# Half of the first MLP product by seven half-size products instead of eight, in blocks 1 to 8

## The chip, the cores and the metric

The kernel runs on one core of one Trainium2 chip. The metric is the device time of one execution in microseconds (us). Three runs before the change took 303.65, 304.41 and 304.56 us, with the median at 304.41 us. The core's engines are named as the profile names them: PE is the matrix engine (TensorE; PEld is its loading of weights), DVE is VectorE, ACT is ScalarE, POOL is GpSimd, and SP issues transfers. SBUF is the on-chip memory. PSUM is the memory into which PE writes its products; the kernel divides it into banks of 512 float32 values in each of 128 partitions.

## What is computed

Sparse attention over 8 batches, 8 heads, 576 positions and head size 64 (four heads with a local window, four with a strided pattern) gives `attn_out`. After it stands an MLP over 4608 tokens, with `d_model` 512 and `d_ff` 2048:

```python
x = attn_out.transpose(0, 2, 1, 3).reshape(B * S, H * D)   # 4608 x 512
h = x @ w_in                                               # MLP1, 512 -> 2048
sp = np.where(h > 20.0, h, np.log1p(np.exp(np.minimum(h, 20.0))))
g = h * np.tanh(sp)                                        # Mish
return (g @ w_out).astype(np.float32)                      # MLP2, 2048 -> 512
```

## The kernel before

Tokens are worked in nine blocks of 512 (`t` = 0 to 8, loop at L758). A block has two stages on PE. In **MLP1** (`mlp1`, L453) a group `g` makes two chunks of 128 rows of `h` transposed: 4 matmuls of 128x512 for each chunk, so 8 for a group, 64 for a block (L473). Mish follows on ACT straight from PSUM into `gT` (L483 for a pair of chunks, L479 for one chunk). In block 4 the 512 tokens wrap around the ring buffer `xT`, so its matmuls are twice as many and half as wide. In **MLP2** of blocks 1 to 8 (`mlp2_seven`, L519, and `mlp2_last`, L588) the product is already made by the Strassen-Winograd scheme: the matrices are cut in quarters, and seven products of quarters with sums of quarters replace eight. Its sums of `g` (`sums_g`, L499, four DVE instructions for a range of chunks, into `Sg`) are made as chunks of `gT` appear, and its sums of `w_out` (`sums_w`, L509, four instructions, into `Tw`) once, in block 1, right after the first piece of MLP1 (L787). Block 0 uses plain products in both stages.

The attention of batch `t + 1` is cut into steps and laid out by hand between the steps of MLP2 of block `t` (`attn_steps`, L391; the list `at` is run at L803). From batch 4 on a few of its last steps go into MLP1 of the next block (`late`, L440). The attention output reaches `xT` by PE transposes and an ACT copy (`xt`, L364): cc 2 and 3 of `xT` hold the strided heads (`X("s", ...)`), cc 0 and 1 the local ones (`X("l", ...)`), which come last.

Everything stands under one manual schedule: each engine takes its instructions in the order in which the program emits them, and an instruction waits until the data and buffers it needs are free. PSUM is divided for blocks 1 to 8 into `acc0` and `acc1` of two banks each, `bank0` and `bank1` of one bank each, and two banks for transposes and small products. MLP1 goes around acc0, acc1 and the bank pair (L460 to L467), so a buffer comes back after two other groups. Of the steps of block 0, the last (`at[15]`, L764) puts on DVE's queue the spreading of V (`spread_v_str`) behind the last attention work, and on POOL's queue the casts of V.

## Time and profile before

| what | before |
|---|---|
| median of 3 runs | 304.41 us |
| the profiled execution, its own time | 303.47 us |
| its span in the profile | 301.7 us |
| MLP1 of block 1, 2, 4, 5, 8, first matmul to the first of MLP2 | 13.94, 13.82, 14.48, 14.11, 13.81 us |
| MLP2 of block 1, 2 (with attention of the next batch) | 17.32, 17.45 us |
| in MLP1 of block 1: DVE, ACT, POOL busy | 11.37, 10.15, 5.61 us |
| in MLP1 of block 2: DVE, ACT, POOL busy | 4.72, 8.26, 2.67 us |

The profile is of one execution, with times from the start of its span. In a row of the timeline stand start, duration, engine, line, operation, what is written and read, the shape, and how many instructions are merged. In a group's row the two numbers behind the bar are busy time in us and the mean of one instruction in ns; behind the next bar stands the idle time of the engine before these instructions and what ended it. Records of matmuls overlap: one of 128x512 shows 379 ns, but the next one starts 216 ns later. What a matmul costs is read from starts.

### The profile page before, as it was taken

The page shows a single profiled execution, that of the slowest core. Times are in us where ns is not written, and L with a number is a line of the kernel's source. Part 1 is how long each engine was busy: PE and PEld are TensorE (multiplying, and loading weights), DVE is VectorE, ACT ScalarE, POOL GpSimd, SP SyncE. Part 2 cuts the span into 40 slices and gives each one's busy share as a digit, 9 for nine tenths or more (in the row PEclk, how much of TensorE's full clock was granted, in tenths as well). Part 3 has the DMA queues.
Part 4 walks back from the last instruction along what each step waited for, and adds up shares of the span by engine and source line. Part 5 has one row for each costly group of instructions (what it writes and reads, how often), then busy time and mean ns, then how long its engine had stood idle before and what let it go on. Part 6 is the DMA issues. An engine that isn't in the chain of part 4 may idle for free.

```text
span 301.7 us, 6848 instructions
## 1 busy us (share of the span) xinstructions
PE 293.5 (97%) x2900; PEld 198.4 (66%) x2921; DVE 156.4 (52%) x356; ACT 171.8 (57%) x220; POOL 108.1 (36%) x116
## 2 busy tenths in 40 slices
PE   8999999999999999999999999999999999999995
PEld 3654555546874688458899885478646864684484
DVE  2360266978561766095617662676348544620732
ACT  1677634587646765567556855675467636404620
POOL 8285302535581239141934085206620510000000
PEclk9999999999999999999999999999999999999999
DMA  8999999969999999999779976994590030003003
GB/s 157 187 202 200 194 197 195 180 132 200 253 156 177 286 175 137 122 272 171 110 133 277 165 94 107 280 146 77 80 243 0 3 141 0 2 0 141 0 0 141
DMA packets 103738, 43.25 MB, mean 143 GB/s; under 512 B 86172, under 2 KB 99212, under 8 KB 103708
## 3 DMA queue, kind: packets, MB, share of 16 engines
q1 hardware_dynamic: 86620, 30.05, 55.9%
q0 software_dynamic: 16800, 12.51, 27.7%
q8 instruction: 23, 0.38, 0.5%
q10 hardware_dynamic: 288, 0.25, 0.3%
q14 instruction: 7, 0.06, 0.1%
HBM read 38.38 MB, written 9.44 MB: 159 GB/s over the span
## 4 chain that ended last, share of the span: by engine, by line
PE 92%; DVE 4%; ACT 2%; issue 1%; ACTq 0%
PE psh L473 32%; PE pso L545 27%; PE psb L473 9%; PE po L333 4%; PE pso L573 4%; PE pso L600 4%; PE ps L303 4%; PE un L257 3%; PE trx L372 2%; PE trx L382 1%; DVE x_l L359 1%; DVE osb L524 1%; PE tr L229 1%; ACT Pl L311 1%; PE tr L243 1%
## 5 line engine op out<-in xcount | busy, mean ns | idle before, releaser
L473 PE MATMUL psh<-xT,w_in 128*128 128x512 bf16 (+1 forms) x484 | 100.7, 358 | 0.8
L473 PEld LDWEIGHTS <-w_in 128*128 128x128 bf16 x640 | 61.5, 98 | 58.3 <-issue 0.8
L483 ACT ACTIVATE gT<-psh 128x1024 bf16<-128x1024 f32 x56 | 56.3, 1023 | 45.4 <-PE psh L473 43.0
L497 DVE TENSOR_TENSOR Sg<-gT 128x256 bf16<-128x256 bf16 (+2 forms) x64 | 29.8, 471 | 50.9 <-ACT gT L483 48.7
L545 PEld LDWEIGHTS <-Sg 128*128 128x128 bf16 x448 | 41.9, 98 | 6.3
L317 POOL TENSOR_TENSOR Pl<-Pl,consts_sb 128x960 bf16<-128x960 bf16 (+1 forms) x18 | 29.2, 1633 | 46.1 <-ACT Pl L311 46.1
L545 PE MATMUL pso<-Tw,Sg 128*128 128x256 bf16 x336 | 40.1, 273 | 0.0
L182 POOL CAST vl<-vl 128x768 bf16<-128x768 f32 x15 | 13.7, 939 | 59.0 <-DMA vl<-in_v_dram 50.5
L545 PEld LDWEIGHTS <-gT 128*128 128x128 bf16 x336 | 31.4, 98 | 4.6
L180 ACT COPY xT<-trx 128x576 bf16<-128x576 bf16 x32 | 20.2, 641 | 19.5 <-PE trx L382 13.6
L473 PE MATMUL psb<-xT,w_in 128*128 128x512 bf16 (+1 forms) x141 | 30.1, 355 | 0.2
L180 ACT COPY osb<-pso 128x512 f32<-128x512 f32 (+1 forms) x26 | 14.2, 545 | 26.4 <-PE pso L545 16.1
L545 PE MATMUL pso<-w_out,gT 128*128 128x256 bf16 x224 | 27.8, 273 | 0.0
L524 DVE TENSOR_TENSOR osb<-pso,osb 128x512 f32<-128x512 f32 x21 | 14.5, 692 | 21.4 <-PE pso L545 21.4
L311 ACT ACTIVATE Pl<-ps 128x960 bf16<-128x960 f32 (+1 forms) x24 | 19.3, 808 | 11.0 <-PE ps L303 10.8
L311 ACT ACTIVATE Ps<-ps 72x864 bf16<-72x864 f32 (+1 forms) x24 | 18.6, 804 | 5.3 <-PE ps L303 5.1
L479 ACT ACTIVATE gT<-psb 128x512 bf16<-128x512 f32 x32 | 19.0, 597 | 2.9 <-PE psb L473 2.5
L359 DVE TENSOR_TENSOR x_s<-po,rden 72x512 bf16<-72x512 f32 x28 | 19.2, 687 | 1.0
L573 PE MATMUL pso<-w_out,gT 128*128 128x512 bf16 x59 | 15.8, 380 | 0.5 <-issue 0.3
L497 DVE TENSOR_TENSOR Sg<-Sg,gT 128x256 bf16<-128x256 bf16 (+2 forms) x32 | 15.6, 488 | 1.1
L344 DVE RECIPROCAL rden<-po 96x4 f32<-96x4 f32 (+1 forms) x22 | 3.9, 178 | 22.1 <-PE po L333 22.0
L333 PEld LDWEIGHTS <-Ps 72*128 72x128 bf16 x256 | 12.1, 97 | 5.0 <-DVE Ps L317 1.9
(89 smaller groups left out, 347.0 us busy)
## 6 DMA issues: line engine op xcount, KB each, us to landing
out_dram<-osb SPq DMA_DIRECT2D x16, 512.0 KB, 6.1
vl<-in_v_dram SPq DMA_DIRECT2D x7, 768.0 KB, 7.4
kl<-in_k_dram SPq DMA_DIRECT2D x6, 576.0 KB, 9.3
ql<-in_q_dram SPq DMA_DIRECT2D x6, 576.0 KB, 13.7
qs<-in_q_dram POOLq DMA_DIRECT2D x8, 288.0 KB, 11.3
vsr<-in_v_dram POOLq DMA_DIRECT2D x8, 288.0 KB, 7.3
w_in<-in_moe_w_in_dram POOLq DMA_DIRECT2D x4, 512.0 KB, 9.7
w_out<-in_moe_w_out_dram POOLq DMA_DIRECT2D x4, 512.0 KB, 17.1
```

The lines of the kernel that those rows point to most:

```text
L180: nc.scalar.copy(out_, in_)
L311: nc.scalar.activation(pt[0:n, :, 0:nw], ps[0:n, :, o0:o0 + nw], AF.Exp, scale=scale)
L317: meng.tensor_tensor(out=pm, in0=pm, in1=mk[0:n, :].unsqueeze(1).unsqueeze(1).to_broadcast([n, 2, nu, w]), op=ALU.mult,)
L333: nc.tensor.matmul(po[:, h, :], lhsT=pt[0:n, c0:c0 + 128], rhs=rhs, start=True, stop=True,)
L359: nc.vector.tensor_tensor(out=dst.rearrange("p e (h d) -> p e h d", h=4), in0=po[0:m, :, :, 0:D], in1=rden[0:m].unsqueeze(3).to_broadcast( ...
L473: nc.tensor.matmul(ps_u[:, o:o + n], lhsT=w_in[:, cc, fc * 128:(fc + 1) * 128], rhs=xT[:, cc, a:a + n], start=(cc == 2 and (o == 0 or len( ...
L479: nc.scalar.activation(gT[:, g + 8 * u, :], ps_u[:], AF.Mish)
L483: nc.scalar.activation(to, tiles[g][:], AF.Mish)
L497: nc.vector.tensor_tensor(out=out_, in0=in0, in1=in1, op=op)
L524: add = lambda o, p: nc.vector.tensor_tensor(out=o, in0=p, in1=o, op=ALU.add)
L545: nc.tensor.matmul(ps[:, pair, :], lhsT=lhs(c, 128 * pair), rhs=rhs(c), start=(first and pair == 0 and c == 0), stop=(last and c == 7), sk ...
L573: nc.tensor.matmul(p[:, ot % 2, :], lhsT=gT[:, fc, 128 * ot:128 * ot + 128], rhs=w_out[:, fc, :], start=(fc == 0), stop=(fc == 15),)
```

## The change

The eight chunks 2 to 5 and 10 to 13 of each block's MLP1 are made by the seven-product scheme, and the other eight by plain groups 0, 1, 6 and 7 as before. The four-chunk *units* are two (n = 0 and 1: chunks 2, 3, 10, 11 and 4, 5, 12, 13). A unit's product is 4 matmuls of 128x256. The two units advance side by side through five stages: `one`, `five`, `two`, `three`, `four`; stage two has two products and stage three has two. Their partial results stay in PSUM: z1 in acc0, z3 in acc1, z2 in the bank pair, and p5 in SBUF. ACT copies z1 to z2 within PSUM, DVE copies z3 to p5 and adds z2 and p5 twice for each unit. The plain group 0 runs between stages two and three. The weights' sums (`sums_w_in`) are made once, at the end of block 0's steps, and three of the four sums of `w_out` are moved to the same place, both ahead of the first of the sums of x for block 1; the fourth sum of `w_out` goes to the last group of block 1. The sums of x (`sums_x`, four DVE instructions of 128x512 for each block) are split: the first in the MLP2 before, the others in MLP1. The sums of `g` are put in another order, and some of them are moved behind the first products of MLP2. To make room, the second buffers of `ql` and `kl` share the memory of `Sw`, later casts and transposes use the first buffer alone, and `Tw` loses a quarter.

```diff
-    ql = [const.tile([128, CL, 4, D], BF16, name=f"ql{i}") for i in range(2)]
-    kl = [const.tile([128, CL, 4, D], BF16, name=f"kl{i}") for i in range(2)]
+    Sw = const.tile([128, 3, 2, 512], BF16, name="Sw")
+    Sx = const.tile([128, 4, 2, 256], BF16, name="Sx")
+    halves = Sw[:].rearrange("p a b c -> p (a b c)").rearrange(
+        "p (z j h d) -> p z j h d", z=2, j=CL, h=4
+    )
+    ql = [const.tile([128, CL, 4, D], BF16, name="ql0"), halves[:, 0]]
+    kl = [const.tile([128, CL, 4, D], BF16, name="kl0"), halves[:, 1]]
...
-    Tw = const.tile([128, 4, 8, 256], BF16, name="Tw")
+    Tw = const.tile([128, 3, 8, 256], BF16, name="Tw")
...
-            to = by_tile(dst[b % 2])
+            to = by_tile(dst[0])
...
-            late = {0: [V("l", 4)], 1: [V("l", 5)], 5: [X("l", 1)]}
+            late = {4: [V("l", 4), V("l", 5)], 6: [X("l", 1)]}
...
-    SUMS_AT = {3: (0, 4), 5: (4, 6), 6: (6, 7), 7: (7, 8)}
-                if t > 0 and g in SUMS_AT:
-                    sums_g(gT, Sg, *SUMS_AT[g])
...
+        z = {}
+
+        def banks():
+            z2 = [bank(u, "psb") for u in range(2)]
+            z1, z3 = [acc(accs[u], "psu") for u in range(2)]
+            p5 = o_pool.tile([128, 2, DM], F32, tag="osb", name="p5")
+            for n in range(2):
+                z[n] = z1[:, n, :], z2[n][:], z3[:, n, :], p5[:, n, :]
+
+        def unit(n):
+
+            f0 = 256 * n
...
+            a11, a12, s3, a22 = [w_quarter(i, j) for i in range(2) for j in range(2)]
+            s1, s2, s4 = [Sw[:, i] for i in range(3)]
+            b11, _, b21, b22 = [x_quarter(t, i, j) for i in range(2) for j in range(2)]
+            t1, t2, t3, t4 = [Sx[:, i] for i in range(4)]
+
+            def product(ps, lhs, rhs, first=False, last=False):
+                for j in range(2):
+                    for cc in range(2):
+                        nc.tensor.matmul(
+                            ps[:, 256 * j:256 * j + 256], lhsT=lhs[:, cc, f0 + 128 * j:f0 + 128 * j + 128],
+                            rhs=rhs[:, cc], start=(first and j == 0 and cc == 0),
+                            stop=(last and cc == 1), skip_group_check=True,
+                        )
+
+            def mish(src, half_f, half_t):
+                c = 8 * half_f + (U0 + f0) // 128
+                nc.scalar.activation(
+                    gT[:, c:c + 2, 256 * half_t:256 * half_t + 256],
+                    src.rearrange("p (j n) -> p j n", j=2), AF.Mish,
+                )
+
+            def one():
+                z1, z2, z3, p5 = z[n]
+                product(z1, a11, b11, first=True)
+                nc.scalar.copy(z2, z1)
+
+            def five():
+                z1, z2, z3, p5 = z[n]
+                product(z3, s1, t1, first=True)
+                nc.vector.tensor_copy(p5, z3)
+
+            def two():
+                z1, z2, z3, p5 = z[n]
+                product(z1, a12, b21, last=True)
+                mish(z1, 0, 0)
+                product(z2, s2, t2)
+                sums(z3, z2, p5, ALU.add)
+
+            def three():
+                z1, z2, z3, p5 = z[n]
+                product(z2, s3, t3)
+                product(z3, s4, b22, last=True)
+                sums(p5, z2, p5, ALU.add)
+                mish(z3, 0, 1)
+                mish(p5, 1, 1)
+
+            def four():
+                z2 = z[n][1]
+                product(z2, a22, t4, last=True)
+                mish(z2, 1, 0)
+
+            return one, five, two, three, four
+
+        one, five, two, three, four = zip(unit(0), unit(1))
+
+        def begin():
+            banks()
+            for f in one:
+                f()
+            sums_x(t, "2")
+            for f in five:
+                f()
+
+        def second():
+            for f in two:
+                f()
+            sums_x(t, "3")
+            sums_x(t, "4")
+
+        def third():
+            for f in three:
+                f()
+
+        def fourth():
+            for f in four:
+                f()
+
+        def plain(g):
+            group(g)
+            if g == 1:
+                sums_g(gT, Sg, 2, 6)
+            if g == 6:
+                sums_g(gT, Sg, 0, 2)
+                sums_g(gT, Sg, 6, 7, "1")
+            if g == 7:
+                if t < B - 1:
+                    nc.scalar.preload_act_table(AF.Exp)
+                if t == 1:
+                    sums_w_last()
+                sums_g(gT, Sg, 7, 8, "1")
+
+        return gT, Sg, [begin, second, lambda: plain(0), third, fourth] + [
+            lambda g=g: plain(g) for g in (1, 6, 7)
+        ]
...
-    def sums_g(gT, Sg, c0, c1):
...
+    def tw_of(i):
+
+        return Tw[:, (0, 1, None, 2)[i]] if i != 2 else w_out[:, 0:8, 256:512]
 
+        sums(tw_of(0), b12, b11, ALU.subtract)
+        sums(tw_of(1), b22, tw_of(0), ALU.subtract)
+        sums(tw_of(3), b21, tw_of(1), ALU.subtract)
+
+    def sums_w_last():
+
+        sums(tw_of(2), w_out[:, 8:16, 256:512], w_out[:, 0:8, 256:512], ALU.subtract)
+
+    U0, U1 = 256, 768
+    GROUP_ACC = {0: 0, 1: 0, 6: 1, 7: 0}
+
+    def w_quarter(i, j):
+
+        return w_in[:, 2 - 2 * j:4 - 2 * j, U0 + 1024 * i:U1 + 1024 * i]
+
+    def sums_w_in():
+
+        a11, a12, a21, a22 = [w_quarter(i, j) for i in range(2) for j in range(2)]
+        s1, s2, s4 = [Sw[:, i] for i in range(3)]
+        sums(s1, a21, a22, ALU.add)
+        sums(s2, s1, a11, ALU.subtract)
+        sums(s4, a12, s2, ALU.subtract)
+        sums(a21, a11, a21, ALU.subtract)
+
+    def x_quarter(t, i, j):
+
+        a = (512 * t + 256 * j) % RT
+        return xT[:, 2 - 2 * i:4 - 2 * i, a:a + 256]
+
+    def sums_x(t, which):
+
+        b11, b12, b21, b22 = [x_quarter(t, i, j) for i in range(2) for j in range(2)]
+        t1, t2, t3, t4 = [Sx[:, i] for i in range(4)]
+        if "1" in which:
+            sums(t1, b12, b11, ALU.subtract)
+        if "2" in which:
+            sums(t2, b22, t1, ALU.subtract)
+        if "3" in which:
+            sums(t3, b22, b12, ALU.subtract)
+        if "4" in which:
+            sums(t4, b21, t2, ALU.subtract)
...
+        steps += product(
+            za, g(0, 0), w(0, 0), True, False,
+            lambda: (cast(nc.vector, c11, za), rest("2")()), late=True,
+        )
+        steps += product(zc, sg(0), tw(0), True, False, lambda: (cast(nc.scalar, c22, zc), rest("4")()))
+        steps += product(za, sg(1), tw(1), False, False, lambda: (cast(nc.scalar, c12, za), rest("3")()))
...
         product(0, g(0, 0), w(0, 0), True, False, lambda n, p: cast(nc.vector, c(0, 0, n), p), late=True)
+        sums_g(gT, Sg, 6, 8, "234")
         product(1, sg(0), tw(0), True, False, lambda n, p: cast(nc.scalar, c(1, 1, n), p))
...
                 at[12].append(load_rest2)
                 at[15] += [
                     lambda: spread_v_str(2, Dv), lambda: cast_v_loc(2, Po),
-                    lambda: load_qk_str(3), lambda: load_early_v_str(3),
+                    lambda: load_qk_str(3), lambda: load_early_v_str(3), sums_w_in, sums_w, lambda: sums_x(1, "1"),
                 ]
...
+                if t + 1 < B:
+                    at[12].append(lambda: sums_x(t + 1, "1"))
...
-                if t == 1 and i == 0:
-                    sums_w()
...
+                if t + 1 == B:
+                    steps[12] = lambda f=steps[12]: (sums_x(t + 1, "1"), f())
```

More of the change, by code (lines that the diff above doesn't have):

```diff
@@ L207, in transpose_by_dma @@
                     dst.rearrange("c (i n) -> c i n", i=NW),
-                    by_tile(src[b % 2])[:, hp].rearrange("p i e d -> p (i e d)"),
+                    by_tile(src[0])[:, hp].rearrange("p i e d -> p (i e d)"),
                 )
@@ L457, in mlp1, with group @@
         held, tiles = {}, {}
-        def group(g, ccs=(2, 3, 0, 1)):
-            single = t > 0 and g % 3 == 2
+        def group(g, ccs=(2, 3, 0, 1), ps=None):
             if g not in held:
-                if single:
-                    held[g] = [bank(u, "psb") for u in range(2)]
-                else:
-                    ps = acc(accs[g % 3], "psh")
-                    held[g] = [ps[:, u, :] for u in range(2)]
-                    tiles[g] = ps
+                if ps is None:
+                    tiles[g] = acc(accs[g % 3 if t == 0 else GROUP_ACC[g]], "psh")
+                    ps = [tiles[g][:, u, :] for u in range(2)]
+                held[g] = ps
             for u in range(2):
@@ L477, in group @@
                         )
-                if ccs[-1] == 1 and single:
-                    nc.scalar.activation(gT[:, g + 8 * u, :], ps_u[:], AF.Mish)
-            if ccs[-1] == 1:
-                if not single:
-                    to = gT[:, g::8, :] if t > 0 else gT[:, 2 * g:2 * g + 2, :]
-                    nc.scalar.activation(to, tiles[g][:], AF.Mish)
-                if t < B - 1 and g == 7:
+                if ccs[-1] == 1 and g not in tiles:
+                    nc.scalar.activation(gT[:, g + 8 * u, :], ps_u, AF.Mish)
@@ L485, in group, with first_group @@
+            if ccs[-1] == 1 and g in tiles:
+                to = gT[:, g::8, :] if t > 0 else gT[:, 2 * g:2 * g + 2, :]
+                nc.scalar.activation(to, tiles[g][:], AF.Mish)
+        if t == 0:
+            def first_group(g):
+                group(g)
+                if g == 7:
                     nc.scalar.preload_act_table(AF.Exp)
-                if t > 0 and g in SUMS_AT:
-                    sums_g(gT, Sg, *SUMS_AT[g])
-        if t == 0:
             halves = [[lambda g=g, c=c: group(g, c) for g in range(3)] for c in ((2, 3), (0, 1))]
-            return gT, halves[0], halves[1] + [lambda g=g: group(g) for g in range(3, 8)]
@@ L491, in mlp1 @@
-        first = [lambda: [group(*x) for x in ((0, (2, 3)), (1, (2, 3)), (0, (0, 1)))], lambda: group(1, (0, 1))]
-        return gT, Sg, first + [lambda g=g: group(g) for g in range(2, 8)]
-    SUMS_AT = {3: (0, 4), 5: (4, 6), 6: (6, 7), 7: (7, 8)}
+            return gT, halves[0], halves[1] + [lambda g=g: first_group(g) for g in range(3, 8)]
+        z = {}
[5 more added lines that the diff above has]
+                z[n] = z1[:, n, :], z2[n][:], z3[:, n, :], p5[:, n, :]
@@ new lines, in plain @@
+        def plain(g):
+            group(g)
+            if g == 1:
[3 more added lines that the diff above has]
+                sums_g(gT, Sg, 6, 7, "1")
+            if g == 7:
+                if t < B - 1:
[6 more added lines that the diff above has]
+        ]
@@ L496, in sums, with sums_g @@
     def sums(out_, in0, in1, op):
         nc.vector.tensor_tensor(out=out_, in0=in0, in1=in1, op=op)
-    def sums_g(gT, Sg, c0, c1):
+    def sums_g(gT, Sg, c0, c1, which="1234"):
         lo1, lo2 = gT[:, c0:c1, 0:256], gT[:, c0:c1, 256:512]
@@ L503, in sums_g @@
         s1, s2, s3, s4 = [Sg[:, i, c0:c1, :] for i in range(4)]
-        sums(s1, lo2, hi2, ALU.add)
-        sums(s2, s1, lo1, ALU.subtract)
-        sums(s4, hi1, s2, ALU.subtract)
-        sums(s3, lo1, lo2, ALU.subtract)
+        if "1" in which:
+            sums(s1, lo2, hi2, ALU.add)
+        if "2" in which:
+            sums(s2, s1, lo1, ALU.subtract)
+        if "3" in which:
+            sums(s3, lo1, lo2, ALU.subtract)
+        if "4" in which:
+            sums(s4, hi1, s2, ALU.subtract)
+    def tw_of(i):
+        return Tw[:, (0, 1, None, 2)[i]] if i != 2 else w_out[:, 0:8, 256:512]
     def sums_w():
@@ L512, in sums_w @@
         b21, b22 = w_out[:, 8:16, 0:256], w_out[:, 8:16, 256:512]
-        t1, t2, t3, t4 = [Tw[:, i] for i in range(4)]
-        sums(t1, b12, b11, ALU.subtract)
-        sums(t2, b22, t1, ALU.subtract)
-        sums(t3, b22, b12, ALU.subtract)
-        sums(t4, b21, t2, ALU.subtract)
+        sums(tw_of(0), b12, b11, ALU.subtract)
[20 more added lines that the diff above has]
+        t1, t2, t3, t4 = [Sx[:, i] for i in range(4)]
+        if "1" in which:
+            sums(t1, b12, b11, ALU.subtract)
+        if "2" in which:
+            sums(t2, b22, t1, ALU.subtract)
+        if "3" in which:
+            sums(t3, b22, b12, ALU.subtract)
+        if "4" in which:
+            sums(t4, b21, t2, ALU.subtract)
     def mlp2_seven(t, gT, Sg, za, zc):
@@ L535, in tw @@
         def tw(i):
-            return lambda c: Tw[:, i, c, :]
+            return lambda c: tw_of(i)[:, c, :]
         def store(h):
@@ L554, in mlp2_seven @@
         cp = lambda eng, o, p: (lambda: cast(eng, o, p))
+        rest = lambda which: (lambda: sums_g(gT, Sg, 6, 8, which))
         steps = []
-        steps += product(za, g(0, 0), w(0, 0), True, False, cp(nc.vector, c11, za), late=True)
-        steps += product(zc, sg(0), tw(0), True, False, cp(nc.scalar, c22, zc))
-        steps += product(za, sg(1), tw(1), False, False, cp(nc.scalar, c12, za))
+        steps += product(
[4 more added lines that the diff above has]
+        steps += product(za, sg(1), tw(1), False, False, lambda: (cast(nc.scalar, c12, za), rest("3")()))
         steps += product(zc, sg(3), w(1, 1), False, True, lambda: add(c12, zc))
@@ L622, in tw @@
         def tw(i):
-            return lambda c: Tw[:, i, c, :]
+            return lambda c: tw_of(i)[:, c, :]
         def done(n, p):
```

## The prediction

> **What bounds the kernel now.** First the page, engines and the chain that ended last:

> ```profile
> PE 293.5 (97%) x2900; PEld 198.4 (66%) x2921; DVE 156.4 (52%) x356; ACT 171.8 (57%) x220; POOL 108.1 (36%) x116
> ...
> PE 92%; DVE 4%; ACT 2%; issue 1%; ACTq 0%
> ```

> PE is the bound nearly everywhere: what shortens its stream shortens the kernel, and what makes it wait lengthens it. The other engines have room on average, so the question is where PE waits. Next the groups of instructions, forms apart (the number before the second bar is the mean in ns):

> ```profile
> L483 ACT ACTIVATE gT<-psh 128x1024 bf16<-128x1024 f32 x56 | 56.3, 1023 | 45.4 <-PE psh L473 43.0 <-PE po L333 2.3
> L479 ACT ACTIVATE gT<-psb 128x512 bf16<-128x512 f32 x32 | 19.0, 597 | 2.9 <-PE psb L473 2.5
> L524 DVE TENSOR_TENSOR osb<-pso,osb 128x512 f32<-128x512 f32 x21 | 14.5, 692 | 21.4 <-PE pso L545 21.4
> L180 ACT COPY osb<-pso 128x512 f32<-128x512 f32 x21 | 12.3, 586 | 16.7 <-PE pso L545 16.1
> ```

> These price the new work: a 128x512 Mish 0.60 us, an addition from PSUM 0.69, a copy 0.59. The timeline of PE in the last block gives the matmul of 128x256:

> ```profile
> 285.90 1.91 PE L600 MATMUL pso<-w_out,gT 128*128 128x256 bf16 x16
> 287.65 3.66 PE L600 MATMUL pso<-Tw,Sg 128*128 128x256 bf16 x32
> 291.14 1.91 PE L600 MATMUL pso<-w_out,Sg 128*128 128x256 bf16 x16
> ```

> From 287.65 to 291.14 are 32 matmuls: 0.109 us each. MLP1 of block 2, 64 of 128x512 in 13.82 us, gives 0.216 each. Last, the passage from block 0 to block 1, first DVE, then PE, then ACT:

> ```profile
> 56.54 0.42 DVE L345 TENSOR_TENSOR x_l<-po,rden 96x256 bf16<-96x256 f32 x1
> 56.88 0.80 DVE L182 COPY vs<-vsr 72x2048 bf16<-72x2048 bf16 x1
> 57.60 1.21 DVE L497 TENSOR_TENSOR Tw<-w_out 128x2048 bf16<-128x2048 bf16 x1
> 58.84 1.73 DVE L497 TENSOR_TENSOR Tw<-w_out,Tw 128x2048 bf16<-128x2048 bf16 x1
> 60.49 1.84 DVE L497 TENSOR_TENSOR Tw<-w_out 128x2048 bf16<-128x2048 bf16 x1
> 62.25 1.84 DVE L497 TENSOR_TENSOR Tw<-w_out,Tw 128x2048 bf16<-128x2048 bf16 x1
> 65.70 0.69 DVE L497 TENSOR_TENSOR Sg<-gT 128x1024 bf16<-128x1024 bf16 x1 [1.61 <-ACT gT L483]
> ```

> ```profile
> 57.41 3.72 PE L473 MATMUL psh<-xT,w_in 128*128 128x512 bf16 x16
> ```

> ```profile
> 60.35 1.28 ACT L483 ACT_TABLE_LOAD   x1 [1.16 <-PE psh L473]
> ```

> DVE goes from attention work straight into the sums of w_out and is busy to 64.1, yet PE starts MLP1 at 57.41 and waits for none of it: before the change nobody needs these sums until MLP2 at 71.35.

> **Step 1, PE's saving.** In a block, 32 matmuls of 128x512 (32 x 0.2157 = 6.90 us) become 2 units x 7 products x 4 = 56 of 128x256 (56 x 0.1091 = 6.11). Saved: 0.79 us; in block 4, whose matmuls are half as wide already, 8 x 0.109 = 0.87. Weight loads hide as in MLP2, where each 128x256 has its own load too.

> **Step 2, new waits inside a block.** Two latencies come from rows like these: PE's 16th matmul has its slot's end at about 80.43, when the next starts, and DVE answers at 80.70, 0.27 later.

> ```profile
> 80.43 0.41 PE L333 MATMUL po<-vs,Ps 72*128 72x65 bf16 x8
> 80.70 0.69 DVE L524 TENSOR_TENSOR osb<-pso,osb 128x512 f32<-128x512 f32 x1 [1.32 <-PE pso L545]
> ```

> Likewise ACT answers PE after 0.20 (MLP1 of block 1 ends at 71.35, its Mish starts at 71.55); PE answers DVE after 0.05 (x_l ends at 149.81, the transposes' load starts at 149.86) and ACT after 0.04 (an Exp ends at 13.87, the product starts at 13.92, 0.04 unrounded). Count from the block's first matmul; a product takes 4 x 0.109 = 0.44. Stages one and five end at 1.75 (first x sum ready earlier, ACT's copies z1 to z2 at 1.6 and 2.1, each before its reader). Stage two: z1 of unit 0 to 2.18, z2 to 2.62, z1 of unit 1 to 3.05, z2 to 3.49. Plain group 0 needs acc0, where z1 sits until its second Mish is done: 3.05 + 0.20 + 0.60 + 0.04 = 3.89, so PE **waits 0.41**. In the old order two groups, 3.45 us, stood between a buffer's uses. Group 0 runs to 5.62. Beneath it DVE finishes its additions and the third and fourth x sum by about 5.1. Stage three runs to 7.37; stage four of unit 1 overwrites z2, which DVE's addition must have read: 6.93 (slot's end of its product) + 0.27 + 0.69 + 0.05 = 7.94, whereas PE comes at 7.80: **0.14**. The remaining 0.44 and three groups of 1.73 end MLP1 at 13.55, against 13.82 before: a net gain of about 0.25 per block. Seven blocks (block 4: 0.87 - 0.55 = 0.32) give 6 x 0.25 + 0.32 = **-1.8 us**.

> Three prices have no row: ACT's copy and DVE's addition that write PSUM from PSUM, and Mish from SBUF. From below they are bounded by zero loss (all waits vanish, -0.8 per block, if nothing is late); from above by taking both PSUM ends in turn, twice 0.59 and 0.69, which makes z1 of both units late by about 0.8 and turns the gain into a loss of 0.5. I take the rows themselves, since only the target differs.

> The rest hides. The sums of g come later and end about 15.1 after the block's start, before MLP2's second product (15.3 at the earliest), because MLP2's first product and its Q steps stand between. The sums moved behind MLP2's first products (0.4 each) fill DVE time in which the first mask waits for Exp. The moved last steps of the attention (`late`) cost PE what they cost now; their DVE work, 1.2 us, ends before stage four's Mish lets the sums of g start. POOL's and SP's queues keep their order; the single buffer of ql and kl is refilled a block after its transposes.

> **Step 3, the passage into block 1.** DVE now does, behind the V copy at 57.6: four sums of w_in (128x1024: 0.69 + 0.73 + 0.73 + 0.61 with overlaps, 2.8), three of w_out (1.24 each, 3.7) and, last, the first sum of x (0.4): 6.9 undisturbed. In the old run the four w_out sums took 6.5 where 4 x 1.24 makes 4.95, since POOL's casts (56.3 to 63.0) ran beside them; these casts stay, so 1.6 is added: the chain ends at 66.1. Stage five's first product needs both the first w_in sum and that last x sum. PE has only stage one (0.87) before it, so it **stands from 58.29 to 66.15**. Then stage five and unit 0's z1 end at 67.46; ACT answers at 67.66, loads its table (1.28, as in the row above, no longer hidden by two groups), does two Mishes, and frees acc0: 70.1. From group 0's start to MLP2 are 9.65: 79.75 instead of 71.35, **+8.4 us**. The chain's end is bounded by 64.5 (no contention) and 68.1 (all stretched by 1.84/1.21).

> How PE comes out of 7.9 us of idleness the trace doesn't show; its longest gap after the start is below 0.2. The nearest row is the start of the span:

> ```profile
> 1.20 6.27 PE L257 MATMUL un<-zeros 128*128 128x512 bf16 x16 [1.20 <-DVE zeros L664]
> ```

> 16 matmuls fill 6.1 us to the next start at 7.30, where 16 x 0.216 is 3.45: a loss of 2.65. So between 0 and 2.65. I take the slow start, because the gap is far nearer to it than to gaps below 0.2, for the 12 matmuls up to unit 0's z1 (12 x 0.11 more): **+1.3**; slowness after that is covered by the wait for the table and Mish. [...]

> [...]

> The fourth w_out sum stands in block 1 ahead of the last sum of g that MLP2's second product needs: 1.24 to 1.84 on a DVE that is already behind, between 0 and 1.2 on PE; I take the middle, **+0.6**.

> **Sum.** 8.4 + 1.3 + 0.6 - 1.8 = +8.5 us: 303.47 + 8.5 = 312.0 for an execution like the profiled one. That one was 0.94 below the median of the runs, so the median is forecast at **312.9**.

> **Rivals.** (a) The block's waits are covered and PE stays fast: 8.4 + 0.6 - 0.80 x 7 = +3.4, 307.8. For it: ACT and DVE have slack on average; against it: acc0 is wanted again 0.44 after z1's last product, less than one Mish. (b) PSUM to PSUM work costs double: 8.4 + 1.3 + 0.6 + 7 x 0.5 = +13.8, 318.2. For it: no such row exists; against: both ends on PSUM need not add up. (c) The other side: PE doesn't stand before stage five of block 1, because the x sum isn't caught behind the weights' sums. Then all eight blocks gain 0.25, -2.1: 302.3. It decides if the chain ends before about 58.9 (8.5 - 1.3 = 7.2 earlier than 66.1). Against it: DVE kept the emitted order in every row above, and the first four sums alone take 2.8 from 57.6. That PE's count doesn't fall is excluded by the shapes.

> **How the numbers follow.** Forecast 0.65, own range 310.5 to 315.3 (the chain's end -1.5 and +1.5, the rest about 1); (a) 0.14, (b) 0.12, (c) 0.07, and 0.02 for a time within 0.3% (about what a measurement tells from no change). The range reaches into (a) and (b): 307.5 to 316.5 leaves out (c), the 0.02 and most of (b). Faster 0.07, same 0.02, slower 0.91.

> **What would show it.** Right: PE idle some 7 to 8 us after 8 matmuls of block 1, released by DVE's x sum, with the rows of w_in and w_out sums before it; matmuls after it at twice the spacing; in later blocks a wait of about 0.4 ahead of group 0 released by Mish and one of 0.1 in stage four released by DVE; MLP1 of block 2 near 13.55. Wrong: PE running through that passage, or MLP1 of block 2 at 13.0 (a) or over 14.2 (b).

## The result and the profile after

The changed kernel takes 331.66 us (median of 4 runs, 331.23 to 331.88) against 304.03: a ratio of 1.091, interval 1.088 to 1.093. The sign was forecast, the size was not: +27.6 us instead of +8.5, far above the stated range of 307.5 to 316.5.

The page of the changed kernel, engines, granted clock and the chain that ended last:

```profile
PE 294.6 (89%) x3059; PEld 214.4 (65%) x3081; DVE 199.5 (61%) x416; ACT 181.9 (55%) x252; POOL 107.1 (33%) x116
...
PEclk9999999679999999999999999999999999999999
...
PE 67%; DMA 12%; ACT 7%; DVE 7%; issue 5%; POOL 2%; DVEq 0%; POOLq 0%; ACTq 0%
```

PE is busy as long as before (294.6 against 293.5 us) in a span that is 27.6 us longer, so the loss is waiting. The clock dips once, in the eighth and ninth slice, where block 1 begins (0.50 granted from 60.38 to 70.62 us). The stages, from the first matmul of one to the first of the next (taken from unrounded starts, so that the last digit can differ by one from the rows), tell where:

| stage | before | after |
|---|---|---|
| MLP1 of block 1 | 13.94 | 24.57 |
| MLP1 of blocks 2, 3 | 13.81 | 16.40 |
| MLP1 of block 4 | 14.49 | 16.82 |
| MLP1 of blocks 5, 6, 7 | 14.11 | 16.74 |
| MLP1 of block 8 | 13.81 | 16.23 |
| MLP2 of block 1, 2 | 17.32, 17.45 | 17.32, 17.42 |
| MLP2 of blocks 4, 5, 6 | 17.38, 17.38, 17.37 | 17.16 |

Block 1 loses 10.6 us, blocks 2 to 8 together 17.8, and MLP2 gives back 0.7. The first was forecast at about 9.7 and 0.6 more in MLP2; for the second 1.8 of gain was forecast. The timeline of PE in block 2, where the forecast has no wait before the one ahead of group 0, the row at 105.55 (a row ends with the idle time before it and who ended it):

```profile
99.12 0.60 PE L513 MATMUL psu<-xT,w_in 128*128 128x256 bf16 x4
100.74 0.60 PE L513 MATMUL psu<-xT,w_in 128*128 128x256 bf16 x4 [1.01 <-ACT psb L529]
101.17 0.60 PE L513 MATMUL psu<-Sx,Sw 128*128 128x256 bf16 x4
102.55 0.60 PE L513 MATMUL psu<-Sx,Sw 128*128 128x256 bf16 x4 [0.78 <-DVE p L534]
102.98 0.60 PE L513 MATMUL psu<-xT,w_in 128*128 128x256 bf16 x4
103.42 0.60 PE L513 MATMUL psb<-Sx,Sw 128*128 128x256 bf16 x4
104.27 0.60 PE L513 MATMUL psu<-xT,w_in 128*128 128x256 bf16 x4 [0.25 <-ACT gT L521]
104.70 0.60 PE L513 MATMUL psb<-Sx,Sw 128*128 128x256 bf16 x4
105.55 1.89 PE L475 MATMUL psh<-xT,w_in 128*128 128x512 bf16 x7 [0.25 <-ACT gT L521]
```

In each stage the second unit starts late. Its first product (100.74) waits for ACT's copy of unit 0's z1, its stage five (102.55) for DVE's copy of unit 0's z3, its stage two (104.27) for unit 0's Mish, although these read the other half of the tile. ACT, in the same stretch:

```profile
100.08 0.60 ACT L529 COPY psb<-psu 128x512 f32<-128x512 f32 x1
101.37 0.57 ACT L529 COPY psb<-psu 128x512 f32<-128x512 f32 x1 [0.68 <-PE psu L513]
103.62 0.60 ACT L521 ACTIVATE gT<-psu 128x512 bf16<-128x512 f32 x1 [1.68 <-PE psu L513]
```

The copy ends at 100.68 and the product starts at 100.74. Read from starts, where a slot is 0.109, the waits of this block are 1.18, 0.95, 0.41, 0.41 (group 0, as forecast) and one of 0.45 in stage three: 3.4 us. Over the whole run, among those who waited for whom:

```profile
PE psu L513 <- ACT psb L529: 7.9, 8, 1.7
...
PE psu L513 <- DVE p L534: 6.3, 8, 0.8
...
PE psu L513 <- DVE Sx L601: 6.0, 1, 6.0
...
PE psu L513 <- ACT gT L521: 4.1, 15, 0.3
```

The numbers are us in all, how often, and the longest. The first two waits come eight times, once in each block; the third row is the single stand in block 1; the fourth joins the waits for Mish in stages two and three. DVE there, then PE:

```profile
57.73 0.67 DVE L601 TENSOR_TENSOR Sw<-w_in 128x1024 bf16<-128x1024 bf16 x1
58.44 1.20 DVE L601 TENSOR_TENSOR Sw<-Sw,w_in 128x1024 bf16<-128x1024 bf16 x1
59.67 1.19 DVE L601 TENSOR_TENSOR Sw<-w_in,Sw 128x1024 bf16<-128x1024 bf16 x1
60.79 1.30 DVE L601 TENSOR_TENSOR w_in<-w_in 128x1024 bf16<-128x1024 bf16 x1
62.02 1.21 DVE L601 TENSOR_TENSOR Tw<-w_out 128x2048 bf16<-128x2048 bf16 x1
63.26 2.48 DVE L601 TENSOR_TENSOR Tw<-w_out,Tw 128x2048 bf16<-128x2048 bf16 x2
65.66 0.42 DVE L601 TENSOR_TENSOR Sx<-xT 128x512 bf16<-128x512 bf16 x1
```

```profile
57.24 0.60 PE L513 MATMUL psu<-xT,w_in 128*128 128x256 bf16 x4
59.56 0.60 PE L513 MATMUL psu<-xT,w_in 128*128 128x256 bf16 x4 [1.72 <-ACT psb L529]
66.14 1.03 PE L513 MATMUL psu<-Sx,Sw 128*128 128x256 bf16 x4 [5.97 <-DVE Sx L601]
```

The chain ends at 66.08 and stage five starts at 66.14; forecast were 66.1 and 66.15. Its first four matmuls fill 1.03 us instead of 0.60: half clock (0.50 granted). ACT's rows show one thing more:

```profile
60.78 1.28 ACT L521 ACT_TABLE_LOAD   x1
69.85 0.60 ACT L521 ACTIVATE gT<-psu 128x512 bf16<-128x512 f32 x1 [7.79 <-PE psu L513]
```

The table for Mish is loaded within the stand, at 60.78, and not behind unit 0's z1 as forecast (67.66); the first Mish starts 0.24 after that product's slot ends (69.61).

### The profile page after: what moved, and what is told of

The parts are those of the page before. It is cut to its first block, busy times and chain, and to the rows that moved or that the text cites. A ratio compares the mean times of both kernels' runs of the same rounds, so it can differ in the third digit from the quotient of the medians.

```text
span 329.3 us, 7289 instructions
## 1 busy us (share of the span) xinstructions
PE 294.6 (89%) x3059; PEld 214.4 (65%) x3081; DVE 199.5 (61%) x416; ACT 181.9 (55%) x252; POOL 107.1 (33%) x116
## 4 chain that ended last, share of the span: by engine, by line
PE 67%; DMA 12%; ACT 7%; DVE 7%; issue 5%; POOL 2%; DVEq 0%; POOLq 0%; ACTq 0%
PE pso L693 26%; PE psh L475 17%; PE psu L513 8%; DMA w_out<-in_moe_w_out_dram 6%; ACT gT L521 4%; PE pso L752 4%; PE po L338 3%; PE ps L308 3%; DMA vl<-in_v_dram 3%; DMA w_in<-in_moe_w_in_dram 3%; PE psb L513 2%; DVE p L534 2%; PE pso L725 2%; ACT osb L185 1%; ACT psb L529 1%
## 5 line engine op out<-in xcount | busy, mean ns | idle before, releaser
L475 PE MATMUL psh<-xT,w_in 128*128 128x512 bf16 (+1 forms) x336 | 72.0, 359 | 3.1 <-ACT gT L521 2.0
L484 ACT ACTIVATE gT<-psh 128x1024 bf16<-128x1024 f32 x40 | 40.8, 1024 | 35.0 <-PE psh L475 35.0
L475 PEld LDWEIGHTS <-w_in 128*128 128x128 bf16 x352 | 33.8, 98 | 34.2 <-issue 4.0
L513 PEld LDWEIGHTS <-w_in 128*128 128x128 bf16 x256 | 25.1, 99 | 16.9 <-issue 12.3
L601 DVE TENSOR_TENSOR Sg<-gT 128x512 bf16<-128x512 bf16 (+2 forms) x56 | 26.1, 467 | 14.1 <-ACT gT L484 8.4
L521 ACT ACTIVATE gT<-psu 128x512 bf16<-128x512 f32 x32 | 19.1, 596 | 26.4 <-PE psu L513 26.4
L513 PEld LDWEIGHTS <-Sw 128*128 128x128 bf16 x192 | 19.1, 100 | 20.2 <-issue 11.5
L185 ACT COPY osb<-pso 128x512 f32<-128x512 f32 (+1 forms) x26 | 14.2, 545 | 26.7 <-PE pso L693 16.4
L513 PE MATMUL psu<-xT,w_in 128*128 128x256 bf16 x128 | 19.7, 276 | 9.7 <-ACT psb L529 7.9
L672 DVE TENSOR_TENSOR osb<-pso,osb 128x512 f32<-128x512 f32 x21 | 14.5, 691 | 20.6 <-PE pso L693 20.6
L693 PE MATMUL pso<-Tw,Sg 128*128 128x256 bf16 x224 | 26.7, 273 | 0.0
L693 PE MATMUL pso<-w_out,Sg 128*128 128x256 bf16 x224 | 26.7, 273 | 0.0
L513 PE MATMUL psu<-Sx,Sw 128*128 128x256 bf16 x64 | 10.4, 289 | 12.2 <-DVE p L534 6.3
L364 DVE TENSOR_TENSOR x_s<-po,rden 72x512 bf16<-72x512 f32 x28 | 19.2, 687 | 1.0
## 6 DMA issues: line engine op xcount, KB each, us to landing
ql<-in_q_dram SPq DMA_DIRECT2D x6, 576.0 KB, 14.5
```

The costliest lines, as they stand in the source:

```text
L185: nc.scalar.copy(out_, in_)
L364: nc.vector.tensor_tensor(out=dst.rearrange("p e (h d) -> p e h d", h=4), in0=po[0:m, :, :, 0:D], in1=rden[0:m].unsqueeze(3).to_broadcast( ...
L475: nc.tensor.matmul(ps_u[:, o:o + n], lhsT=w_in[:, cc, fc * 128:(fc + 1) * 128], rhs=xT[:, cc, a:a + n], start=(cc == 2 and (o == 0 or len( ...
L484: nc.scalar.activation(to, tiles[g][:], AF.Mish)
L513: nc.tensor.matmul(ps[:, 256 * j:256 * j + 256], lhsT=lhs[:, cc, f0 + 128 * j:f0 + 128 * j + 128], rhs=rhs[:, cc], start=(first and j == 0 ...
L521: nc.scalar.activation(gT[:, c:c + 2, 256 * half_t:256 * half_t + 256], src.rearrange("p (j n) -> p j n", j=2), AF.Mish,)
```

## The experiments

Theory 1, formed from this trace: two independent causes. In every block a PSUM tile of two banks is waited for as a whole, so unit 1 waits until unit 0's half has been read. In block 1, DVE's queue holds all the weights' sums ahead of the x sum. Rivals: the new work of ACT and DVE is too slow whatever the tiles are, or one cause stands behind both. Lengths are of MLP1 unless said otherwise.

| kernel | time | ratio to before, interval | block 1, and its MLP2 | block 2 |
|---|---|---|---|---|
| changed kernel | 331.66 | 1.091, 1.088 to 1.093 | 24.57, 17.32 | 16.40 |
| a_split | 311.21 | 1.023, 1.021 to 1.026 | 23.72, 17.32 | 13.50 |
| b_sums_later | 329.35 | 1.082, 1.079 to 1.085 | 21.47, 18.73 | 16.40 |
| c_split_sums_later | 306.16 | 1.007, 1.005 to 1.010 | 16.47, 19.24 | 13.50 |
| d_warm | 330.32 | 1.087, 1.085 to 1.089 | 23.33, 17.54 | 16.40 |
| e_reorder | 303.21 | 0.995, 0.993 to 0.997 | 17.86, 19.03 | 13.05 |
| f_staged | 299.79 | 0.986, 0.984 to 0.988 | 15.12, 17.74 | 13.39 |
| g_interleave | 324.92 | 1.068, 1.067 to 1.070 | 24.57, 17.32 | 15.40 |
| h_earlier | 299.01 | 0.985, 0.982 to 0.987 | 13.64, 17.74 | 13.40 |

**a_split.** The pools of acc0 and acc1 are closed and opened anew around the stages, so that the same four banks are four tiles while the units use them:

```diff
-            z1, z3 = [acc(accs[u], "psu") for u in range(2)]
+            reopen(0, 1)     # close the pools of acc0, acc1 and open them anew
+            z1, z3 = [[half(accs[u], n, "psu") for n in range(2)] for u in range(2)]
...
-                z[n] = z1[:, n, :], z2[n][:], z3[:, n, :], p5[:, n, :]
+                z[n] = z1[n][:], z2[n][:], z3[n][:], p5[:, n, :]
```

> Each unit's z1 and z3 get tiles of one bank of their own, in the same PSUM places; nothing else changes. Theory 1 (a tile of two banks is waited for as a whole: unit 1's writes wait for the reading of unit 0's half): the waits ahead of unit 1 in stages one, five, two and three go, 1.0 to 1.2, 0.8 to 0.9, 0.4 and 0.4 us for each block, MLP1 of block 2 falls from 16.40 to about 13.55, block 1 by about 1, and the time to about 311. Rival (the new work on ACT and DVE is too slow for PE whatever the tiles, or the neighbouring bank itself delays the write): MLP1 of block 2 stays at 16.4 and the time at 331.

Measured: 311.21, MLP1 of block 2 at 13.50. PE in block 2 of this kernel:

```profile
99.35 1.04 PE L536 MATMUL psu<-xT,w_in 128*128 128x256 bf16 x8
100.23 1.04 PE L536 MATMUL psu<-Sx,Sw 128*128 128x256 bf16 x8
101.10 0.60 PE L536 MATMUL psu<-xT,w_in 128*128 128x256 bf16 x4
101.54 0.60 PE L536 MATMUL psb<-Sx,Sw 128*128 128x256 bf16 x4
101.97 0.60 PE L536 MATMUL psu<-xT,w_in 128*128 128x256 bf16 x4
102.41 0.60 PE L536 MATMUL psb<-Sx,Sw 128*128 128x256 bf16 x4
103.26 1.89 PE L497 MATMUL psh<-xT,w_in 128*128 128x512 bf16 x8 [0.25 <-ACT gT L544]
```

Both units run on without a gap; of the waits in these rows only the one ahead of group 0 is left. Sizes and the reading engines are as they were. The places are not quite, against what the expectation says: the pools are opened in another order, so z1 lies in banks 6 and 7 instead of 0 and 1, and z3 in 4 and 5 instead of 2 and 3; but the two halves of each are neighbours as before. So neither slow readers nor a neighbouring bank made these waits: the shared tile did. The program itself holds them. In the changed kernel unit 1's first matmul in stages one, five, two and three is given a semaphore to wait for, which ACT or DVE raises after reading unit 0's half; in a_split it has none in stages one, five and three, and in stage two it waits only for the copy of its own z1. 20.5 us of the 27.6 are gone.

**b_sums_later and c_split_sums_later.** The second stands on a_split.

```diff
-                    ..., sums_w_in, sums_w, lambda: sums_x(1, "1"),
+                    ..., lambda: sums_x(1, "1"), sums_w_in,
...
+                if t == 1 and i == 4:
+                    sums_w()
```

> Two-bank tiles as in the changed kernel; at the end of block 0 the first sum of x stands first, then the four sums of w_in; the three sums of w_out stand behind stage four of block 1. Theory 1 (the stand of 6.0 us ahead of stage five in block 1 is DVE's queue): that stand nearly goes, PE isn't idle long enough for a lower clock, MLP1 of block 1 falls from 24.57 to about 17, some 1 us is given back in the sums of g; time about 325. Rival (the stand comes from something else, such as transfers or POOL's casts beside DVE): MLP1 of block 1 stays above 23.

> Both edits together. Theory 1: the gains add, about 331.7 - 20.5 - 6.5 = 304.5, within 1.5 of the kernel before: what the seven products save is then used up by the two waits that are left in a block (0.41 ahead of group 0, 0.14 in stage four) and by block 1. Rival (one cause behind both, so that the second edit brings nothing more): as a_split, about 311.

Measured: 329.35, a gain of 2.3 instead of 6.5, and with a_split 306.16, a gain of 5.1 on it. The stand ahead of stage five is indeed gone, but in b_sums_later another comes in its place, as DVE and then PE show:

```profile
61.97 1.04 DVE L601 TENSOR_TENSOR Sx<-xT,Sx 128x512 bf16<-128x512 bf16 x1
62.93 0.68 DVE L534 COPY p<-psu 128x512 f32<-128x512 f32 x1
```

```profile
60.04 0.60 PE L513 MATMUL psu<-Sx,Sw 128*128 128x256 bf16 x4
63.66 1.01 PE L513 MATMUL psu<-Sx,Sw 128*128 128x256 bf16 x4 [3.02 <-DVE p L534]
```

Stage five of unit 0 runs at 60.04, but DVE's copy of its z3 stands behind the w_in sums and the second x sum until 62.93, and unit 1 waits for that copy through the shared tile. The granted clock was 0.50 from 62.84 to 69.67, where the expectation had no lower clock. So the causes are separate, but their gains don't add: alone they bring 20.5 and 2.3, together 25.5, since in b_sums_later the shared tile passes DVE's delay on to unit 1. With tiles of their own the next wait, 2.2 us, is the second x sum itself, and the late w_out sums cost 1.9 in MLP2 of block 1. The sum of 304.5 was missed by 1.7. In the profiled executions block 1 with its MLP2 is 5.3 shorter than in a_split instead of 6.5, and blocks 2 to 8 are the same.

**d_warm.** In the changed kernel, within the stand:

```diff
             for f in one:
                 f()
+            if t == 1:
+                unread(26)
```

> The changed kernel with 26 products of zeros, which nobody reads, 5.6 us of PE's time put into its stand ahead of stage five of block 1. Theory 1 (PE's clock falls because PE stands): the granted clock stays at 1.0 there, DVE's chain ends as before, and MLP1 of block 1 is 1.3 to 2.0 shorter; time about 330. Rival (the fall is not tied to the stand, or costs nothing since other waits cover it): MLP1 of block 1 stays at 24.5.

Measured: 330.32, MLP1 of block 1 shorter by 1.24 (a little under the 1.3 to 2.0 expected; its MLP2 is 0.22 longer), granted clock 1.0 all through it, against a mean of 0.79 in the changed kernel. PE:

```profile
59.93 5.78 PE L262 MATMUL un<-zeros 128*128 128x512 bf16 x26
66.15 0.60 PE L513 MATMUL psu<-Sx,Sw 128*128 128x256 bf16 x4 [0.45 <-DVE Sx L603]
```

Stage five starts at the same moment as in the changed kernel, but at full pace (0.60 instead of 1.03). The half clock in block 1 costs 1.2 us, and the stand is its cause: with 5.78 us of products in it the clock stays at 1.0. In this execution the clock fell once elsewhere, to 0.50 from 135.48 to 138.89 in block 3, whose MLP1 took 17.50 us.

**g_interleave.** The changed kernel with its two-bank tiles; only the order of the first four products is another:

```diff
-            for f in one: ...
-            for f in five: ...
+            one[0](); five[0](); one[1]()
+            sums_x(t, "2")
+            five[1]()
```

> The changed kernel with its two-bank tiles; only the first four products stand in another order: stage one and five of unit 0, then those of unit 1. Theory 1 (unit 1's writes wait until unit 0's half of the same tile is read): the wait ahead of unit 1's stage one falls by 0.4 and the one ahead of its stage five from 0.9 to nearly nothing, since another product stands between; MLP1 of block 2 from 16.40 to about 15.1, time about 321. Rival (the waits are tied to the place in the stage, not to the tile): 16.4 and 331.

Measured: 324.92, MLP1 of block 2 at 15.40. PE there:

```profile
100.41 0.60 PE L513 MATMUL psu<-Sx,Sw 128*128 128x256 bf16 x4
101.58 0.60 PE L513 MATMUL psu<-xT,w_in 128*128 128x256 bf16 x4 [0.57 <-ACT psb L529]
102.01 0.60 PE L513 MATMUL psu<-Sx,Sw 128*128 128x256 bf16 x4
102.83 0.60 PE L513 MATMUL psu<-xT,w_in 128*128 128x256 bf16 x4 [0.22 <-ACT psb L529]
```

The wait ahead of unit 1's stage one (101.58) falls from 1.18 to 0.74 and the one ahead of its stage five (102.01) is gone, as a product stands between the writer and the reader. A wait of 0.38 comes in, ahead of unit 0's stage two (102.83), for ACT's copy of unit 1's z1, which is the other half of the tile; hence 1.0 per block instead of 1.3. The waits follow the tile, not the stage, and here the tiles lie where they lay.

**e_reorder, f_staged and h_earlier** build on c_split_sums_later. The first takes the second products of stages two and three into a step of their own:

```diff
-            for f in two:
+            for f in two + two_b:        # z1, z1, z2, z2
...
-            for f in three:
+            for f in three + three_b:    # z2, z2, z3, z3
```

The second deals out block 1's sums:

```diff
-                    lambda: spread_v_str(2, Dv), ..., sums_w_in,
+                    lambda: spread_v_str(2, Po), ..., lambda: sums_w_in((0, 1, 3)),
...
+                at[12].append(lambda: Sc.preload_act_table(AF.Mish))
...
+            if t == 1:
+                sums_w_in((2,))          # between the third and the fourth x sum
...
+                    sums_w((0,))         # behind stage four of block 1
+                    at[5].append(sums_w_last)
+                    at[7].append(lambda: sums_w((3,)))
```

The third moves two of them into MLP2 of block 0:

```diff
-                    ..., lambda: sums_w_in((0, 1, 3)),
+                    ..., lambda: sums_w_in((3,)),
...
+                at[9].append(lambda: sums_w_in((0,)))
+                at[10].append(lambda: sums_w_in((1,)))
```

> As c_split_sums_later, but stages two and three take the products of both units by turns: z1, z1, z2, z2 and z2, z2, z3, z3. Theory 1 (what is left in a block is the answering time: 0.41 us for Mish behind z1 ahead of group 0, nothing else): z1 of unit 1 ends 0.44 earlier, the wait goes, MLP1 of block 2 falls from 13.50 to about 13.05, that is 8 x 0.45 = 3.6 less, time about 302.5, below the kernel before. Rival (another wait takes its place, since z2 is then later by as much for DVE): MLP1 of block 2 stays at 13.5 and the time at 306.

> As e_reorder, and in block 1 each sum of weights stands on DVE's queue just ahead of its first reader instead of all at once: first x sum and three w_in sums, then the fourth in stage two, two w_out sums behind stage four, the last two within MLP2; V's copy goes to POOL, ACT's table for Mish is loaded in MLP2 of block 0. Theory 1 (block 1's loss is only the order on DVE's queue): MLP1 of block 1 from 16.5 to about 13.5 and its MLP2 from 19.2 to about 17.6, time about 298. Rival (the sums' 7 to 8 us of DVE time can't be hidden there, because DVE is the bound of that stretch): at most 1 less than e_reorder.

> As f_staged, with the first two w_in sums moved into MLP2 of block 0, behind its steps 9 and 10, where DVE has gaps of 0.8 us between attention work; the fourth stays at the end of the steps. Theory 1 (what is left in block 1 is the second x sum behind three w_in sums on DVE, 1.4 us of waiting, and 0.3 each ahead of stages five and two): the wait falls to below 0.3, MLP1 of block 1 from 15.1 to about 13.8, MLP2 of block 0 grows by at most 0.4; time about 298.8. Rival (DVE is full there, so that the attention steps are pushed by as much as MLP1 gains): MLP2 of block 0 grows by a us or more and the time stays at 299.8.

Measured: 303.21, 299.79 and 299.01. MLP1 of block 2 is 13.05 in e_reorder, the 0.45 that was expected; 8 x 0.45 is 3.6, yet the median falls by 3.0 only. The profiled execution, with a mean granted clock of 0.994, has half clock in block 1 (0.50 from 63.23 to 66.65; MLP1 of 17.86 instead of 16.47); six more of the twelve runs show the same mean clock, and the five at 0.998 or more have a median of 302.1. In f_staged MLP1 of block 1 takes 15.12 instead of the 13.5 expected: it keeps one long wait, 1.4 us from starts, and two of 0.3, and DVE's rows show why the rival's reason held in part there:

```profile
58.60 1.20 DVE L632 TENSOR_TENSOR Sw<-Sw,w_in 128x1024 bf16<-128x1024 bf16 x1
59.72 1.30 DVE L632 TENSOR_TENSOR w_in<-w_in 128x1024 bf16<-128x1024 bf16 x1
60.95 1.04 DVE L632 TENSOR_TENSOR Sx<-xT,Sx 128x512 bf16<-128x512 bf16 x1
```

```profile
62.04 1.03 PE L536 MATMUL psb<-Sx,Sw 128*128 128x256 bf16 x8 [1.19 <-DVE Sx L632]
```

DVE was full between 57 and 62. f_staged also moves the copy of V to POOL and loads ACT's table earlier; what each of these edits brings alone was not run. In h_earlier the wait for DVE is gone and one of 0.6 for ACT's copy is left at that place: MLP1 of block 1 falls to 13.64, MLP2 of block 0 keeps its 22.15, and the kernel, with the same seven products, is 1.6% faster than before (0.985, interval 0.982 to 0.987). From block 3 on its MLP1 takes 0.55 to 0.85 us less than before, in blocks 5 to 7, with the 0.55, after an MLP2 that is 0.22 shorter: what step 1 promised and no more.

## Why the prediction was wrong

- **What bounds the kernel and step 1** were right: in e_reorder, where nearly no wait is left in a block, MLP1 of block 2 is 13.05 against 13.81, 0.76 of the 0.79 reckoned.
- **Step 2 is the step that failed.** It took the units as independent ("Stages one and five end at 1.75 ..., ACT's copies z1 to z2 at 1.6 and 2.1, each before its reader") and looked for waits only between a product and the reader of the same bank. The program waits for the whole tile: 1.18, 0.95 and 0.41 in stages one, five and two, and 0.45 in stage three. So the term of -1.8 for blocks 2 to 8 was measured at +17.8. The forecast 13.55 for MLP1 of block 2 was 16.40, and 13.50 once the tiles were apart (a_split), whose time of 311.21 lies inside the forecast's own range of 310.5 to 315.3 (in part by luck, see step 3). The rows of MLP1 before could not show it: there a group writes both halves before one instruction reads both. But it was not listed as an unknown, and so the range had no room for it; the time that rival (b) gave, 318.2, was too short as well.
- The wait ahead of group 0 was right (0.41 of 0.41); the one in stage four, 0.14, is 0.07 in a_split and 0 in the changed kernel, where PE comes later (row at 109.47).
- **The prices without a row** were right. Groups of the changed kernel:

```profile
L601 DVE TENSOR_TENSOR psu<-psb,p 128x512 f32<-128x512 f32 x16 | 11.2, 700 | 7.0 <-PE psb L513 7.0
...
L521 ACT ACTIVATE gT<-p 128x512 bf16<-128x512 f32 x16 | 10.0, 627 | 0.0
...
L529 ACT COPY psb<-psu 128x512 f32<-128x512 f32 x16 | 9.2, 577 | 5.6 <-PE psu L513 5.5
```

  700, 627 and 577 ns stand against 692, 597 and 586 taken: both ends in PSUM cost nothing more, and rival (b)'s mechanism is out.
- **Step 3** was right to 0.1 us in the end of DVE's chain and in the start of stage five, though all of the loss put down to POOL's casts, carried over from the w_out sums of before, fell on the w_in sums (4.3 us instead of 2.8, and 3.6 instead of 3.7 for w_out). It was wrong on ACT's table: the load, reckoned behind unit 0's z1, lay in the stand and cost PE nothing. About 0.9 of the 8.4 rested on it, since without the load group 0 would start 3.02 after stage five as in other blocks, at 69.17 instead of 70.1. That MLP1 of block 1 is 23.72 in a_split, against 13.94 + 8.4 + 1.3 = 23.6, is therefore partly luck: from stage five on it takes 14.61 there, 1.99 more than the 12.62 of block 2, the clock being halved from 61.26 to 71.50, where the forecast had 0.9 for the table and 1.3 for the clock; and stage five starts 9.11 after the block's start instead of 8.74. In the changed kernel the clock's price was 1.24 (d_warm). The fourth w_out sum, taken at 0.6, cost nothing: MLP2 of block 1 is 17.32 before and after.
- On contention, the two chained w_in sums beside POOL's casts (56.44 to 61.55) took 1.20 and 1.19, where a sum of this shape takes 0.69 alone: a partial loss of 0.5, as in the rows of before (1.73 and 1.84 against 1.21). The first w_in sum, beside the same casts, took 0.67 and lost nothing, so that no rule comes out of these rows.

## What to carry to other kernels

Before work on two halves of a tile is called independent, look for a place where one half is written while the other is still read; here the program tracks tiles as a whole, and four such places were waits of 1.18, 0.95, 0.41 and 0.45 us in a block. Separate tiles took them out (a_split); another product between write and read took out the 0.95, left 0.74 of the 1.18 and brought one of 0.38 (g_interleave). Work that is done once still stands on a queue (here PE stood 5.97 us behind it): put each such instruction ahead of its first reader and not ahead of everybody else's. Before a saving of 6% on a stage is counted on, see that every stage behind it has its answers ready: here 0.79 us per block needed five waits out of the way first.

## What the runs showed of the hardware

```profile
132.07:135.48 3.41, 1.62 (x14) 1.15 (x12) 1.64 (x2) 1.92 (x4) 2.34 (x2) 1.00 0.61 119
135.48:138.89 3.41, 3.41 (x18) 2.39 (x17) 1.39 (x2) 0.75 (x2) 0.00 (x0) 0.50 1.01 162
```

The first columns are the stretch, its length and PE's busy time; the third from the end is the granted clock. In the changed kernel's block 2, where PE was busy for about 2.4 us of 3.4, it did not fall, nor behind 200.33 to 203.74 us, with 1.79. The busy share alone doesn't decide: in the kernel before, 1.57 us from 296.72 to 300.13, at the end of the run, was followed by a granted clock of 1.00. The four falls came behind stretches that were 30 to 47% busy (1.03 to 1.62 us). How a wait lies to the stretches differed between these executions. c_split_sums_later waits 2.2 us at the same place without a fall: a stretch laid over that wait, 59.20 to 62.60, has only 1.03 us of PE, but counted from that execution's first rise (6.49 us) the wait is shared by two stretches with 2.36 and 1.74:

```profile
57.69:61.10 3.41, 2.36 (x19) 1.57 (x17) 3.34 (x5) 3.39 (x6) 2.62 (x2) 1.00 1.30 122
61.10:64.51 3.41, 1.74 (x14) 1.31 (x14) 3.41 (x6) 1.52 (x3) 1.98 (x2) 1.00 0.91 178
```

e_reorder's runs go with it: the seven with a mean granted clock of 0.994, which one halved stretch in 301.6 us makes, took 303.05 to 304.06, and the five at 0.998 to 1.0 took 300.66 to 302.23. What spreads the times within each group is open.
